# The last expert's product 128 rows wide, joined to the spreading product: attention and a soft mixture of experts on one core

## The chip, the cores and the metric

One Trainium2 chip, one core of it. The metric is device microseconds per execution; the kernel before takes 178.54 us (median of three runs, 178.18 to 178.70). One execution was profiled. An expert's weights are 4 MB as float32; the kernel casts them to 16 bits while loading.

## The reference

Windowed attention (8 batches, 8 heads, 576 positions, head size 64; half of the heads see the last 32 positions, half every fourth of the last 128) feeds a soft mixture of 8 experts with 4 slots each. What matters here is the second part, with x of 4608 rows and 512 columns:

```python
logits = x @ phi                              # 4608 x 32 slots
slot_input = softmax(logits, over rows).T @ x # 32 x 512
for e in range(8):
    h = maximum(slot_input[e] @ w1[e], 0)     # 4 x 1024
    slot_out[e] = h @ w2[e]                   # 4 x 512
return softmax(logits, over slots) @ slot_out # 4608 x 512
```

All of x must be seen before the experts can start, and all experts before the first row of the result.

## The kernel before

The order of the work on each engine is the order in which the program issues it (a manual schedule). A loop over the batches pipelines the attention by a hand-written list of steps; in it GpSimd (POOL) issues the loads of q, k, v and, between them, the weights. All these transfers and the outputs go through one software DMA queue, in order of issue. w1 of all experts and w2 of experts 0 to 2 are loaded during the loop. When the raw inputs of the last batch have been read (L550), their memory becomes the pool `w2b`: one transfer brings w2 of experts 3, 4 and 5 (3 MB as 16-bit numbers), and experts 6 and 7 go into the freed q/k slabs, first the columns 0 to 255 of both, then the columns 256 to 511; expert 7's come in two transfers each, chunks 0 to 3 and 4 to 7 (`load_half`, L216 to L220).

The hidden values are computed 32 columns per expert (`hps`, L608), transposed to `hT`, and copied to `hTm` (L620 for experts 0 to 3 on DVE, L623 for 4 to 7 on ACT). In `hTm` each expert has 32 columns, of which only its own 4 slots are not zero.

The second layer (`emit_so`, L635 to L648) multiplies, for each of 8 chunks of 128 hidden values, these 32 columns with the chunk of w2. A product fills 32 of the 128 columns of TensorE's array, and four products are put at four different column groups: experts 0 to 3 side by side, and for a single expert chunk c goes to rows 32*(c%4) of the accumulator `so`. So `so` holds four partial sums of the 32 slots. `gather_so` (DVE) copies half of its columns to `so_part` as 16-bit numbers; `spread_so` multiplies them with the constant `spread`, which adds the four partial sums and at the same time writes the sum to all four groups of 32 rows; ACT copies this to `so_sb`.

```python
so[row : row + 32, cols],
hTm[:, g, c, 32 * j : 32 * j + 32],
w2t[e][:, c, cols],
```

Then the output. `emit_fin` (L662) multiplies 128 rows of the exponentials ET (32 slots) with `so_sb`; the four row groups of `so_sb` serve four such blocks of a batch at four row groups of the array. The products go to `psum_f`, with four buffers. ACT (L673) and DVE (L677) take turns to scale a block into `om`. `emit_batch` does the four blocks of a batch and issues its output on POOL (L686). Six batches are written in two halves of the columns: `emit_so(0, ...)`, gather and spread for columns 0 to 255 come first; the loop over the six batches writes these columns, and expert 6's second half is put ahead of batch 2, expert 7's ahead of batch 4, the gather ahead of batch 5, the spread behind batch 5. Then come the second halves of the six batches, two whole batches, and the last 64 rows of each batch (`om_l`, L713).

Of the kernel before, what the change touches and what calls it, by code (L numbers as in the profile page):

```python
# [9 lines left out]
FP32 = mybir.dt.float32  # L10
FP16 = mybir.dt.float16
# [29 lines left out]
DH = DMODEL // 2  # L41
# [55 lines left out]
def kernel(  # L97
# [10 lines left out]
    nc = tc.nc  # L108
# [10 lines left out]
    spread = cst[:, o + 128 : o + 256]  # L119
# [10 lines left out]
    so_part = consts.tile([128, DMODEL], FP16, name="so_part")  # L130
    so_sb = consts.tile([128, DMODEL], FP16, name="so_sb")
    hTm = consts.tile([128, 2, 8, 128], FP16, name="hTm")
# [3 lines left out]
    w1t, w2t = {}, {}  # L136

    def weights_tile(pool, which, e0, e1):
        n = (4 * FDIM, 8 * DMODEL)[which - 1]
        t = pool.tile([128, e1 - e0, n], FP16, name=f"w{which}_{e0}", tag=f"w{which}_{e0}")  # L140
        for e in range(e0, e1):
            of = t[:, e - e0]
            if which == 1:
                w1t[e] = of.rearrange("p (c f) -> p c f", c=4)
            else:
                w2t[e] = of.rearrange("p (c n) -> p c n", c=8)
        return t
# [16 lines left out]
    def slab_weights(e, tag, n):  # L164
        t = fix.tile([128, n], FP16, name=f"w2_{e}", tag=tag)
        w2t[e] = t[:, 0 : 8 * DMODEL].rearrange("p (c n) -> p c n", c=8)
# [9 lines left out]
    ring = ctx.enter_context(tc.tile_pool(name="ring", bufs=2, space=bass.MemoryType.PSUM))  # L176
# [28 lines left out]
    def load_full(t, which, e0, e1):  # L205
        if which == 1:
            nc.gpsimd.dma_start(
                out=t.rearrange("p e (u x) -> p (e u) x", u=2),
                in_=moe_w1[e0:e1].rearrange("e (u p c) f -> p (e u) (c f)", u=2, p=128),
            )  # L210
        else:
            nc.gpsimd.dma_start(
                out=t, in_=moe_w2[e0:e1].rearrange("e (p c) n -> p e (c n)", p=128)
            )

    def load_half(e, s, n):  # L216
        src = moe_w2[e].rearrange("(p c) n -> p c n", p=128)
        cols = slice(DH * s, DH * s + DH)
        for u in range(0, 8, n):
            nc.gpsimd.dma_start(out=w2t[e][:, u : u + n, cols], in_=src[:, u : u + n, cols])  # L220
# [249 lines left out]
    for which in "QK":  # L470
        load_raw(which, 1)
    nc.gpsimd.dma_start(
        out=phi_raw.rearrange("p (u c) s -> p u (c s)", u=2),
        in_=moe_phi.rearrange("(u p c) s -> p u (c s)", u=2, c=2),
# [15 lines left out]
    def step(op, b):  # L490
        if op[0] in "ARM" and op[1:] in TILES:
            kind, i = TILES[op[1:]]
            if op[0] == "A":
                tmp[(op[1:], b)] = emit_av(b, kind, i)
            elif op[0] == "R":
                tmp[("R" + op[1:], b)] = emit_recip(b, kind, i, tmp[(op[1:], b)])
            else:
                engine = nc.scalar if op[1:] in ON_ACT else nc.vector
                norm_mult(b, kind, i, tmp.pop((op[1:], b)), tmp.pop(("R" + op[1:], b)), engine)
        elif op in ("S0", "S1", "S2"):  # L500
            tmp[(op, b)] = emit_scores(b, int(op[1]))
        elif op in ("E0", "E1", "E2"):
            emit_exp(b, int(op[1]), tmp.pop(("S" + op[1], b)))
        elif op in ("MK0", "MK1", "MK2"):
            emit_mask(b, int(op[2]))
        elif op[0:2] in ("QT", "KT", "VT"):
            turn(op[0], b, int(op[2]))
        elif op in ("XP0", "XP1"):
            tmp[(op, b)] = xT_plain(b, int(op[2]))
        elif op in ("XD0", "XD1"):  # L510
            tmp[(op, b)] = xT_dil(b, int(op[2]))
        elif op in ("XPc0", "XPc1", "XDc0", "XDc1"):
            xT_copy(b, op[1], int(op[3]), tmp.pop((op[0:2] + op[3], b)))
        elif op in ("VA", "VB", "VC", "VD"):
            tmp[(op, b)] = v_rows(b, "ABCD".index(op[1]))
        elif op in ("VAc", "VBc", "VCc", "VDc"):
            v_place(b, "ABCD".index(op[1]), tmp.pop((op[0:2], b)))
        elif op in ("LG", "EP"):
            tmp[(op, b)] = (back_logits if op == "LG" else back_erow)(b)
        elif op == "ET":  # L520
            back_et(b, tmp.pop(("LG", b)))
        elif op == "ER":
            back_er(b, tmp.pop(("EP", b)))
        else:
            {"ED": back_erd, "U": back_u, "UT": back_add}[op](b)

    def loads(which, b):
        load_raw(which, b)
        if which == "V":
            if b > 2:  # L530
                load_weights(1)
            if b == B - 1:
                load_weights(len(weights))
# [5 lines left out]
    w2b_pool = None  # L539
    for it in range(B + max(s for _, s in STEPS)):  # L540
        for op, stage in STEPS:
            b = it - stage
            if not 0 <= b < B:
                continue
            step(op, b)
            if op in frees and b + 2 < B:
                loads(frees[op], b + 2)
            left.discard((op, b))
            if w2b_pool is None and not left:
                raw_pool.release()  # L550
                w2b_pool = tc.alloc_tile_pool(name="w2b", bufs=1, side="right")
                late = weights_tile(w2b_pool, 2, 3, 6)
                slab_weights(6, "qk0", QK_SLAB)
                slab_weights(7, "qk1", QK_SLAB)
                load_full(late, 2, 3, 6)
                for s in range(2):
                    for e in (6, 7):
                        load_half(e, s, 8 if e == 6 else 4)
        if it == 0:
            nc.vector.tensor_copy(  # L560
                out=phi4, in_=phi_raw[:, :, None, :].broadcast_to([128, 4, 4, N_SLOTS])
            )
# [6 lines left out]
    h_pool = tc.alloc_tile_pool(name="hp", bufs=1)  # L569
# [33 lines left out]
    for fc in range(2):  # L603
        for g in range(2):
            for dc in range(4):
                for j in range(4):
                    e = 4 * g + j
# [4 lines left out]
                        start=(g == 0 and dc == 0),  # L612
                        stop=(g == 1 and dc == 3),
# [3 lines left out]
    for c in range(8):  # L617
# [3 lines left out]
        out=hTm[:, 0].rearrange("p c (j s) -> p c j s", j=4)[:, :, :, 0:16], in_=hT4[:, :, :, 0:16]  # L621
    )
    nc.scalar.copy(  # L623
        out=hTm[:, 1].rearrange("p c (j s) -> p c j s", j=4)[:, :, :, 16:32], in_=hT4[:, :, :, 16:32]
    )
    psum_e.release()
    psum_f = tc.alloc_tile_pool(name="psum_f", bufs=4, space=bass.MemoryType.PSUM)

# [6 lines left out]
    def emit_so(s, experts):  # L635
        cols = slice(0, DMODEL) if s is None else slice(DH * s, DH * s + DH)
        for c in range(8):
            for e in experts:
                g, j = divmod(e, 4)
                row = 32 * (j if len(experts) == 4 else c % 4)  # L640
                nc.tensor.matmul(
                    so[row : row + 32, cols],
                    hTm[:, g, c, 32 * j : 32 * j + 32],
                    w2t[e][:, c, cols],
                    start=(e < 4 and c == 0),
                    stop=(e == 7 and c > 3),
                    skip_group_check=True,
                )  # L648

    def gather_so(s):  # L650
        cols = slice(DH * s, DH * s + DH)
        nc.vector.tensor_copy(out=so_part[:, cols], in_=so[:, cols])

    def spread_so(s):
        cols = slice(DH * s, DH * s + DH)
        rep = ring.tile([128, DH], FP32, name=f"rep_{s}", tag="ring")
        nc.tensor.matmul(rep, spread, so_part[:, cols], start=True, stop=True)
        nc.scalar.copy(out=so_sb[:, cols], in_=rep)

    turn = [0]  # L660

# [19 lines left out]
    def emit_batch(b, c0, c1, n=4):  # L681
        dst = out[S * b : S * b + 512].rearrange("(j p) d -> p j d", p=128)
        for j0 in range(0, 4, n):
            for j in range(j0, j0 + n):
                emit_fin(et_cols(b)[0], j, c0, c1, om[b][:, j, c0:c1], 4 * b + j)
            nc.gpsimd.dma_start(  # L686
                out=dst[:, j0 : j0 + n, c0:c1], in_=om[b][:, j0 : j0 + n, c0:c1]
            )
# [2 lines left out]
    emit_so(None, (0, 1, 2, 3))  # L691
    for e in (4, 5):
        emit_so(None, (e,))
    for e in (6, 7):
        emit_so(0, (e,))
    gather_so(0)
    spread_so(0)
    for b in range(NHALF):
        if b in (2, 4):
            emit_so(1, ({2: 6, 4: 7}[b],))  # L700
        if b == 5:
            gather_so(1)
        emit_batch(b, 0, DH, 2 if b == 0 else 4)
    spread_so(1)
    for b in range(NHALF):
        emit_batch(b, DH, DMODEL)
    for b in range(NHALF, B):
# [4 lines left out]
    for e in range(2):  # L712
        nc.gpsimd.dma_start(  # L713
            out=rest[:, e, 512:576, :].rearrange("n i d -> i n d"), in_=om_l[64 * e : 64 * e + 64]
# [37 lines left out]
```

## Time and profile before

| | |
|---|---|
| median of three runs | 178.54 us |
| the profiled execution's own time | 178.29 us |
| its span, first to last instruction | 176.5 us |
| PE, DVE, ACT busy | 123.5, 126.0, 123.5 us |
| POOL busy | 38.4 us |
| read from and written to HBM | 62.07 and 9.44 MB |
| first output issued | 149.40 us |
| last two outputs issued from | 166.34 us |

The profile gives one page for an execution: the span in 40 slices, with each engine's busy tenths, the clock granted to TensorE (PEclk) and what the DMA engines moved; the chain of work that ended last; and groups of instructions by source line. Lnnn is a line of the kernel. The trace behind it can be asked for windows of time, for a tile's instructions, for waits, and for each DMA's time from issue to landing. All times below are microseconds from the start of the span.

### The profile page before, as it was taken

Reading aid. Unit: us, or ns where it says so; the run is one execution under the profiler, and the core shown is the slowest. Engines: PE = TensorE matmul, PEld = TensorE weight load, DVE = VectorE, ACT = ScalarE, POOL = GpSimd, SP = SyncE. Lnnn points to the kernel's source line nnn. Section 1 sums busy time; section 2 is a strip of 40 time slices with the busy share of each in tenths; the row PEclk is TensorE's granted clock in tenths of the full one; section 3 lists DMA queues with packets and bytes.
Section 4 is the critical chain, followed back from the end, with each engine's and each line's share of the span. In section 5 each row is a group of like instructions: output and inputs, shape, how many; then the busy total and the mean of one; then the engine's idle time right before and its main releaser. Section 6 shows DMA issues by size and latency. Waiting matters only on the chain.

```text
span 176.5 us, 4724 instructions
## 1 busy us (share of the span) xinstructions
PE 123.5 (70%) x2004; PEld 80.9 (46%) x2004; DVE 126.0 (71%) x275; ACT 123.5 (70%) x266; POOL 38.4 (22%) x60
## 2 busy tenths in 40 slices
PE   0026928998888888988989888978677295778300
PEld 0015616676566566656766557656332142221000
DVE  6473899999999999999999998465130104878500
ACT  6007758999999999999999999995501104888300
POOL 7321022112112112116000002710000001856600
PEclk9999999969999999999789999996858969655555
DMA  5999999999999999999999999999999999999997
GB/s 83 215 214 210 214 212 215 215 213 214 216 212 217 211 218 215 208 215 220 213 211 217 213 218 216 222 210 225 213 213 221 192 198 175 340 398 397 401 415 209
DMA packets 18981, 40.83 MB, mean 231 GB/s; under 512 B 1169, under 2 KB 11537, under 8 KB 18193
## 3 DMA queue, kind: packets, MB, share of 16 engines
q0 software_dynamic: 18816, 40.41, 113.8%
q8 instruction: 15, 0.25, 0.5%
q1 hardware_dynamic: 144, 0.14, 0.3%
q14 instruction: 6, 0.04, 0.1%
HBM read 62.07 MB, written 9.44 MB: 405 GB/s over the span
## 4 chain that ended last, share of the span: by engine, by line
ACT 38%; DMA 27%; DVE 14%; PE 10%; issue 2%; POOL 2%; POOLq 0%; ACTq 0%
DMA w<-in_moe_w_dram 19%; ACT p L282 10%; DMA phi_raw<-in_moe_phi_dram 8%; ACT vX L253 7%; ACT xp L337 7%; DVE qk L231 5%; PE f L664 5%; ACT om L673 3%; ACT xT L376 3%; ACT xT L378 3%; DVE p L293 3%; DVE vT L231 3%; ACT xd L337 2%; PE s L273 2%; PE rp L357 2%
## 5 line engine op out<-in xcount | busy, mean ns | idle before, releaser
L282 ACT ACTIVATE p<-s 128x1920 f16<-128x1920 f32 (+1 forms) x24 | 44.6, 1857 | 10.2 <-PE s L273 10.1
L273 PE MATMUL s<-qk 32*128 32x128 f16 (+2 forms) x704 | 26.7, 295 | 18.4 <-DVE qk L231 12.0
L253 ACT COPY vX<-rv 128x768 f16<-128x768 f16 (+1 forms) x32 | 27.8, 943 | 1.8 <-PE rv L247 1.8
L316 PEld LDWEIGHTS <-p 128*128 128x128 f16 (+1 forms) x480 | 22.4, 103 | 13.3 <-DVE xp L341 4.0
L337 ACT ACTIVATE xp<-o_P,rc_P 128x64 f16<-128x64 f32 x96 | 26.5, 497 | 2.2 <-DVE rc_P L328 2.2
L273 PEld LDWEIGHTS <-qk 32*128 32x128 f16 x704 | 17.3, 117 | 21.6 <-DVE qk L231 12.0
L293 DVE TENSOR_TENSOR p<-p,masks 128x1920 f16<-128x1920 f16 (+1 forms) x24 | 25.7, 1084 | 0.2
L231 DVE STREAM_TRANSPOSE qk<-rawQ 128x576 uint32<-128x576 uint32 x16 | 18.8, 1243 | 2.7 <-DMA rawQ<-in_q_dram 2.7
L316 PE MATMUL o_P<-vX,p 128*128 128x65 f16 (+1 forms) x288 | 20.0, 205 | 0.8 <-ACT xp L337 0.2
L231 DVE STREAM_TRANSPOSE qk<-rawK 128x576 uint32<-128x576 uint32 x16 | 19.5, 1231 | 0.4 <-DMA rawK<-in_k_dram 0.4
L247 PE MATMUL rv<-cst,vT 128*128 128x128 f16 x176 | 17.5, 242 | 3.2 <-DVE vT L231 1.8
L231 DVE STREAM_TRANSPOSE vT<-rawV 128x576 uint32<-128x576 uint32 x16 | 19.4, 1223 | 0.5 <-DMA rawV<-in_v_dram 0.5
L686 POOL DMA_DIRECT2D out_dram<-om x15 | 11.1, 744 | 39.2 <-DVE om L677 34.8
L247 PEld LDWEIGHTS <-vT 128*128 128x128 f16 x176 | 13.2, 124 | 7.5 <-issue 3.7
L677 DVE TENSOR_SCALAR om<-f,rrow 128x256 f16<-128x256 f32 (+1 forms) x28 | 13.5, 519 | 3.5 <-PE f L664 2.9
L664 PE MATMUL f<-so_sb,ET 32*128 32x256 f16 (+1 forms) x60 | 12.5, 392 | 3.9 <-ACT om L673 2.7
L673 ACT ACTIVATE om<-f,rrow 128x256 f16<-128x256 f32 (+1 forms) x28 | 12.8, 503 | 2.6 <-PE f L664 2.0
L376 ACT COPY xT<-rp 128x576 f16<-128x576 f16 x16 | 11.5, 909 | 1.3 <-PE rp L357 1.3
L316 PE MATMUL o_D<-vX,p 128*128 128x65 f16 x128 | 9.9, 202 | 2.5 <-DVE xp L341 2.0
L201 POOL DMA_DIRECT2D rawQ<-in_q_dram x8 | 5.1, 633 | 29.4 <-DVE rc_P L328 18.4
L378 ACT COPY xT<-rd 128x576 f16<-128x576 f16 x16 | 10.6, 795 | 0.0
L341 DVE TENSOR_TENSOR xd<-o_D,rc_D 128x256 f16<-128x256 f32 x24 | 9.9, 412 | 0.2
(81 smaller groups left out, 176.7 us busy)
## 6 DMA issues: line engine op xcount, KB each, us to landing
w<-in_moe_w_dram POOLq DMA_DIRECT2D x3, 3072.0 KB, 35.5
out_dram<-om POOLq DMA_DIRECT2D x11, 512.0 KB, 4.6
w<-in_moe_w_dram POOLq DMA_DIRECT2D x5, 1024.0 KB, 15.9
rawQ<-in_q_dram POOLq DMA_DIRECT2D x8, 576.0 KB, 12.7
rawK<-in_k_dram POOLq DMA_DIRECT2D x8, 576.0 KB, 11.4
rawV<-in_v_dram POOLq DMA_DIRECT2D x8, 576.0 KB, 11.6
out_dram<-om POOLq DMA_DIRECT2D x2, 1024.0 KB, 7.3
w<-in_moe_w_dram POOLq DMA_DIRECT2D x2, 512.0 KB, 36.7
```

The source lines that it names most:

```text
L231: nc.vector.transpose(out=out_, in_=in_)
L247: nc.tensor.transpose(rg[:, n_t, :, c, :], rows, ident)
L253: copy(out=vX[b % 2][:, t0 : t0 + n, :, 0:D], in_=rg.rearrange("p n h c d -> p n h (c d)"))
L273: nc.tensor.matmul(sps[:, h, c0 : c0 + w], kk, qq, start=(tt == 0), stop=(tt == 1))
L282: return nc.scalar.activation(out=pt, in_=sps[:, :, 0:n], func=AF.Exp, scale=SCALE)
L293: return nc.vector.tensor_tensor(out=pt, in0=pt, in1=m, op=ALU.mult)
L316: nc.tensor.matmul(o[rows, h, :], lhs, rhs, start=(n == 0), stop=(n == len(jobs) - 1), skip_group_check=True,)
L337: nc.scalar.activation(out=dst[:, h], in_=src[:, h], func=AF.Copy, scale=rc[:, h : h + 1])
L376: copy(out=xT_t[b][:, c, :], in_=rg[:, 0:S])
L378: copy(out=xT_t[b][:, 2 + c, :].rearrange("p (i r) -> p i r", r=DIL), in_=rg[:, :, 0:SUB].rearrange("p r i -> p i r"),)
L664: nc.tensor.matmul(fp[:, 0 : c1 - c0], ET[32 * j : 32 * j + 32, m : m + 128], so_sb[32 * j : 32 * j + 32, c0:c1], start=True, stop=True,)
L673: nc.scalar.activation(out=dst, in_=fp[:, 0 : c1 - c0], func=AF.Copy, scale=rrow[:, blk : blk + 1])
```

## The change

Three things are done.

First, the transfer of w2 of experts 3, 4 and 5 becomes two: expert 3 alone, then 4 and 5.

Second, a tile `hT7` holds expert 7's hidden columns four times side by side, so that its products are 128 wide: each fills all columns of the array and writes the same 32 sums to all four row groups.

Third, expert 7 leaves `emit_so`. `gather_so` now gathers the other seven experts and issues the spreading product at once, into an accumulation that it leaves open; `last_so` adds expert 7's eight products to it and copies the sum to `so_sb`. For the columns 0 to 255 the two stand one after the other ahead of the first batch. For the columns 256 to 511 expert 6 and the gather stand ahead of batch 2, and `last_so` behind batch 3.

```diff
-                late = weights_tile(w2b_pool, 2, 3, 6)
+                late = {x: weights_tile(w2b_pool, 2, *x) for x in ((3, 4), (4, 6))}
...
-                load_full(late, 2, 3, 6)
+                for x, t in late.items():
+                    load_full(t, 2, *x)
...
+    hT7 = h_pool.tile([128, 8, 4, 32], FP16, name="hT7", tag="hT7")
+    nc.vector.tensor_copy(out=hT7, in_=hTm[:, 1, :, None, 96:128].broadcast_to([128, 8, 4, 32]))
...
-                    stop=(e == 7 and c > 3),
+                    stop=(e == 6 and c > 3),
...
+    rep = {}
 
     def gather_so(s):
         cols = slice(DH * s, DH * s + DH)
         nc.vector.tensor_copy(out=so_part[:, cols], in_=so[:, cols])
 
-    def spread_so(s):
+        rep[s] = ring.tile([128, DH], FP32, name=f"rep_{s}", tag="ring")
+        nc.tensor.matmul(rep[s], spread, so_part[:, cols], start=True, stop=False)
+
+    def last_so(s):
         cols = slice(DH * s, DH * s + DH)
-        rep = ring.tile([128, DH], FP32, name=f"rep_{s}", tag="ring")
-        nc.tensor.matmul(rep, spread, so_part[:, cols], start=True, stop=True)
-        nc.scalar.copy(out=so_sb[:, cols], in_=rep)
+        for c in range(8):
+            nc.tensor.matmul(
+                rep[s],
+                hT7[:, c].rearrange("p a s -> p (a s)"),
+                w2t[7][:, c, cols],
+                start=False,
+                stop=(c == 7),
+            )
+        nc.scalar.copy(out=so_sb[:, cols], in_=rep[s])
...
-    for e in (6, 7):
-        emit_so(0, (e,))
+    emit_so(0, (6,))
     gather_so(0)
-    spread_so(0)
+    last_so(0)
     for b in range(NHALF):
-        if b in (2, 4):
-            emit_so(1, ({2: 6, 4: 7}[b],))
-        if b == 5:
+        if b == 2:
+            emit_so(1, (6,))
             gather_so(1)
         emit_batch(b, 0, DH, 2 if b == 0 else 4)
-    spread_so(1)
+        if b == 3:
+            last_so(1)
```

## The prediction

> **What bounds the kernel now.** I read the page first, its slices in time above all:
>
> ```profile
> PE   0026928998888888988989888978677295778300
> DMA  5999999999999999999999999999999999999997
> GB/s 83 215 214 210 214 212 215 215 213 214 216 212 217 211 218 215 208 215 220 213 211 217 213 218 216 222 210 225 213 213 221 192 198 175 340 398 397 401 415 209
> ```
>
> The DMA row is full from the second slice to the last, while every engine has gaps. So whatever the change does to an engine must be asked twice: does it move the end of the DMA stream? Next, the chain of waits over the stretch that the change edits:
>
> ```profile
> 112.33 34.05 DMA w<-in_moe_w_dram
> 146.37 0.04 issue
> 146.41 0.32 PE so L641 x4
> ...
> 146.76 0.43 DVE so_part L652
> ...
> 147.23 0.28 PE rep L657
> ...
> 147.54 0.38 ACT so_sb L658
> ...
> 147.96 0.31 PE f L664 x4
> ```
>
> Read alone, this says that from the landing of expert 7's second quarter (146.37) to so_sb (147.92) lie 1.55 us, of which gather and spreading product are some 0.8. Then DMA by stretches of time (last two numbers: DMA share, GB/s):
>
> ```profile
> 140.00:149.00 9.00, 5.68 (x68) 2.71 (x68) 1.07 (x3) 1.11 (x3) 0.00 (x0) 0.81 1.42 193
> 149.00:149.50 0.50, 0.50 (x8) 0.11 (x7) 0.50 (x2) 0.50 (x3) 0.10 (x1) 1.00 0.96 130
> 149.50:150.00 0.50, 0.50 (x12) 0.21 (x12) 0.50 (x2) 0.43 (x2) 0.50 (x1) 1.00 0.76 101
> 150.00:150.50 0.50, 0.39 (x4) 0.17 (x3) 0.29 (x2) 0.37 (x1) 0.50 (x2) 1.00 0.63 86
> 150.50:151.00 0.50, 0.34 (x2) 0.18 (x2) 0.50 (x2) 0.50 (x3) 0.50 (x2) 1.00 1.31 232
> 151.50:166.00 14.50, 10.87 (x54) 2.85 (x53) 12.24 (x25) 11.37 (x24) 9.01 (x13) 0.50 1.97 396
> ```
>
> There is a trough between the weights and the outputs, about 1 us deep. It looks like the prize, but the packet records of the trace show who idles in it. Each transfer ends with 16 four-byte completion writes, one per DMA engine. Nine engines write their last of the weights by 149.9; seven go on, the last until 151.41. That slowest engine then completes the outputs at 152.06, 152.71, 154.01, 155.31, 156.62, 157.94 and so on to 174.78: 0.65 us per 256 KB and 1.31 per 512 KB throughout, the pace of the full stream. It never waits for an output, and it ends last. So the end is its weights plus its share of the outputs; an earlier first output fills the trough of the other nine only. What counts for the end is that no output comes late for the slowest engine. POOL issues them so:
>
> ```profile
> 149.40 3.03 POOL L686 DMA_DIRECT2D out_dram<-om  x4 [33.97 <-DVE om L677]
> 152.63 0.74 POOL L686 DMA_DIRECT2D out_dram<-om  x1 [0.19 <-issue]
> 153.95 0.74 POOL L686 DMA_DIRECT2D out_dram<-om  x1 [0.57 <-ACT om L673]
> 155.06 0.75 POOL L686 DMA_DIRECT2D out_dram<-om  x1 [0.37 <-issue]
> ```
>
> The first packet of an output starts at 150.68, 1.28 us after its issue. The slack of an output is thus the slowest engine's previous completion less issue plus 1.28: 0.7 us for the first three, 1.0 for batch 2, 1.4 for batch 3 and 1.39 for batch 4 (issued 153.95, wanted 156.62 - 1.28 = 155.34).
>
> **The change part by part.** *w2 of expert 3 alone.* One more POOL issue, 0.77 us (the row of L212). It pushes expert 6's first half from 106.34 to 107.1; POOL then idles 4.3 us until 111.58 in any case, and the transfers wait some 34 us in the queue, which hides it. Without that cover it would cost 0.77. On the stream: two 256 KB pieces take the slowest engine 2.68 us where one 512 KB piece takes 2.65, so 0.03. Expert 3 lands at about 131 (126.47, the landing before, plus a third of the 14.6 us to 141.1). So the 32 products of experts 0 to 3 run at 138.44 and no longer wait until 141.15.
>
> *hT7.* A DVE copy of 128x1024, bounded by the 128x512 copies: 2 x 0.29 (L560) to 2 x 0.42 (L620); I take 0.8, as it stands next to the latter. It waits for ACT's copy (139.0) and ends by 139.9; DVE has no other work until the gather, 144.2 now, and the first reader starts at 145. Hidden.
>
> *Join ahead of the landing, columns 0 to 255.* Expert 6's half lands at 143.73 (106.34 + 37.4), its products end by 144.15, gather 0.43, spread 0.28: done at 144.9, before expert 7's quarters (145.04 and 146.37). After the second quarter four products are left. They are 128 wide, and where before four 32-wide ones started within 0.02 us of each other (146.41 to 146.43), these take turns: 256 columns are 0.107 us each at full clock, 0.213 at half (512 columns: groups start 0.213 and 0.427 apart). With the tail of 0.17 that is 0.59 or 1.02, so_sb ends at 147.41 or 147.84 instead of 147.91: 0.50 or 0.07 earlier. By the slowest engine this is worth 0.0.
>
> *Columns 256 to 511.* Here it costs. Expert 7's eight products were two groups, 0.43 us at half clock; now they are eight turns, 1.71. They stand behind batch 3 in PE's queue, ahead of batch 4's products, and the copy to so_sb now stands ahead of batch 4 on ACT (0.37). And at batch 2, PE's queue holds the spreading product, which waits for a gather that DVE reaches only behind batch 1's evictions; batch 2's products stand behind it. The later gather, product and copy after batch 5 go away, but there the queue has slack.
>
> *Which clock.* Granted clock in the gate's own stretches (PE busy, clock):
>
> ```profile
> 140.87:144.28 3.41, 3.13 (x32) 0.50 1.45 197
> 144.28:147.70 3.42, 2.04 (x38) 1.00 1.45 198
> 147.70:151.11 3.41, 2.35 (x23) 1.00 1.13 164
> 151.11:154.52 3.41, 2.55 (x19) 0.50 1.92 389
> ```
>
> The clock of a stretch follows the array work of the one before, counted as columns times the filled share of the array: 2,944 (144.28 to 147.70) kept it full; 2,769 (31.64 to 35.06) and 1,472 (147.70 to 151.11) lost it. After the change the stretch from 140.87 holds experts 4, 5 and 6 alone: 16 x 128 + 8 x 64 = 2,560, so it should be half from 144.28.
>
> [...]
>
> *The sum at half clock.* With rows of before (evictions 0.37 apart on ACT and 0.41 on DVE, 0.47 long; POOL 0.53 behind the last eviction, as 153.42 to 153.95): batch 1's evictions and the gather end at 150.45; spread, then batch 2's products from 150.8, evicted 151.2 to 152.1; batch 3 152.1 to 153.05; the eight products 152.37 to 154.07; their tail and the copy end at 154.65; batch 4 is evicted by 155.49 and issued at 156.02, 0.68 after 155.34. If the clock is full again from 147.70 to 151.11, the same steps give 155.56, 0.22 late; full throughout, 154.29, 1.05 early. The same chain for before gives 153.79 (153.95 in the trace). Outputs behind batch 4 keep 0.3 us or more. I take the middle of the two half-clock cases, 0.45: the profiled execution's 178.29 (span 176.5 and 1.8 around it) + 0.45 + 0.03 = 178.77; its time stands 0.25 below the median of the three runs, so 179.0 beside 178.54. Bounds: nothing to 0.9 late, by the 0.2 us of drift in that chain.
>
> **The rivals.** *No change, 178.5.* Batch 4 comes in time: full clock, or slack that the chain counts too small. For it: the other free-running stretches could begin elsewhere; the slack at half clock is missed by only 0.2 to 0.7. It decides at an issue of 155.34.
>
> *The first output decides: faster, 178.0.* If the end follows the nine engines that idle in the trough, so_sb's 0.50 at full clock is gained; the whole trough, 0.96, is the limit (177.6). For it: 86 GB/s at 150.0. Against: the completions of the slowest engine, without a gap.
>
> *Weight loads of 128 columns show.* If the eight loads of 0.10 us (L657's) don't run beside the products, batch 4 is 0.8 later still: 178.54 + 0.45 + 0.8 = 179.8. Against: transposes at L357 start 0.055 apart with a load of 128 columns each.
>
> **How the numbers follow.** About 0.3%, 0.54 us, can be told from no change. Batch 4 late: 0.52, of which 0.31 above 0.54 and 0.21 below. Loads show: 0.12, all slower. No change: 0.18. First output decides: 0.18, of which 0.13 beyond 0.54. Slower 0.31 + 0.12 = 0.43; same 0.21 + 0.18 + 0.05 = 0.44; faster 0.13. The range 178.0 to 179.7 leaves out most of the loads' case and the deep end of the faster one; the likeliest case alone gives 178.5 to 179.4.
>
> **What would show it.** Right: PE clock 0.5 in 144.3 to 147.7; eight products at the new line between batch 3 and 4 taking about 1.7 us; batch 4's output issued after 155.3; a dip of GB/s near 156 to 157; the landing of the last weight at 151.7 as before. Wrong: clock full there, or batch 4 issued before 155 with no dip (no change); a stream that ends 0.5 earlier with the same landing of the weights (first output decides). A last weight landing that moves by itself would upset every step, since all is counted from it.

## The result, and the profile after

The changed kernel takes 179.63 us (median of six, 179.35 to 180.08) against 178.29 for the kernel before on the same chip (178.11 to 178.70): 1.0075 times as long, 95% interval 1.0055 to 1.0094. That is 1.34 us slower. The profiled execution took 179.35 us, with a span of 177.6.

The path that the change was cut for did get shorter. The chain of waits after the change, from the landing of expert 7's second quarter on:

```profile
146.06 0.04 issue
146.11 1.03 PE rep L665 x4
147.13 0.02 issue
147.16 0.38 ACT so_sb L672
147.54 0.04 issue
...
149.91 0.44 DVE so_part L657
150.35 0.04 issue
150.40 0.37 PE rep L660
150.77 0.37 PE f L678 x3
...
152.46 1.82 PE rep L665 x8
```

From the landing to the end of the copy to so_sb it is now 1.48 us instead of 1.55: gather and spreading product are gone from it, but the four 128-wide products take 1.03 instead of 0.32. Further down stand the two new waits: the gather and the spreading product ahead of batch 2 (149.91 to 150.77), and eight products, 1.82 us, ahead of batch 4. What they do to the outputs shows in POOL's instructions after the change:

```profile
149.07 2.17 POOL L700 DMA_DIRECT2D out_dram<-om  x3 [21.94 <-DVE om L691]
152.57 0.75 POOL L700 DMA_DIRECT2D out_dram<-om  x1 [1.32 <-ACT om L687]
153.51 0.75 POOL L700 DMA_DIRECT2D out_dram<-om  x1 [0.20 <-issue]
156.07 0.74 POOL L700 DMA_DIRECT2D out_dram<-om  x1 [1.82 <-ACT om L687]
157.01 0.74 POOL L700 DMA_DIRECT2D out_dram<-om  x1 [0.20 <-ACT om L687]
```

The first output is issued earlier (149.07 instead of 149.40, though only 0.02 earlier against the landing of the last weight, of which more below), but batch 2's only at 152.57 (before, the last of the four issues from 149.40, at 151.69) and batch 4's at 156.07 (before: 153.95). After each of them the DMA stream has a hole. Stretches of time after the change, DMA share and GB/s last:

```profile
151.50:153.00 1.50, 1.35 (x7) 0.68 (x7) 1.41 (x4) 1.31 (x4) 0.43 (x1) 0.50 1.91 387
153.00:153.50 0.50, 0.50 (x4) 0.36 (x3) 0.00 (x0) 0.00 (x0) 0.31 (x1) 0.50 1.14 223
153.50:154.00 0.50, 0.50 (x4) 0.23 (x2) 0.00 (x0) 0.00 (x0) 0.49 (x1) 0.50 0.46 96
154.00:156.50 2.50, 1.83 (x13) 0.65 (x12) 1.75 (x4) 2.02 (x6) 0.68 (x2) 0.50 1.98 403
156.50:157.00 0.50, 0.40 (x3) 0.14 (x2) 0.45 (x2) 0.50 (x2) 0.32 (x1) 0.50 0.14 19
157.00:157.50 0.50, 0.49 (x3) 0.20 (x3) 0.42 (x2) 0.41 (x2) 0.49 (x1) 0.50 0.28 66
157.50:166.00 8.50, 7.32 (x31) 1.56 (x28) 7.53 (x15) 7.68 (x16) 5.45 (x8) 0.50 1.98 400
```

Before the change there was no such hole between 151.5 and 166. By the completion writes in the packet records, the slowest engine stood still for 0.36 us ahead of batch 2's output and for 0.89 us ahead of batch 4's.

The trace's landing times sum it up in one number per kernel, the time from the last weight's landing to the last output's landing: 151.70 to 175.23 before, 23.53 us; 151.38 to 176.28 after, 24.90 us. The outputs take 1.37 us longer, and the profiled execution is 1.06 slower because its weights happened to land 0.32 earlier. I use this length, called the output phase, for all experiments below.

| kernel | median us | ratio to before (95%) | output phase, us |
|---|---|---|---|
| before | 178.29 | | 23.53 |
| the change | 179.63 | 1.0075 (1.0055 to 1.0094) | 24.90 |
| first half of the columns alone | 178.15 | 0.9993 (0.9984 to 1.0002) | 23.54 |
| second half alone | 179.70 | 1.0077 (1.0061 to 1.0092) | 25.24 |
| expert 3 alone | 178.16 | 0.9996 (0.9987 to 1.0004) | 23.54 |
| eight products behind batch 5 | 179.89 | 1.0083 (1.0062 to 1.0103) | 25.26 |
| join and products behind batch 5 | 179.73 | 1.0069 (1.0048 to 1.0089) | 24.23 |
| eight products more | 181.95 | 1.0201 (1.0182 to 1.0220) | 27.76 |
| fillers that keep the clock | 179.85 | 1.0069 (1.0045 to 1.0092) | 26.12 |
| five fillers ahead of the first output | 179.13 | 1.0050 (1.0028 to 1.0072) | 23.90 |
| ten fillers there | 181.08 | 1.0148 (1.0132 to 1.0164) | 26.67 |
| one more copy on ACT | 178.42 | 1.0002 (0.9990 to 1.0014) | 23.79 |
| four more copies on ACT | 179.13 | 1.0051 (1.0030 to 1.0072) | 24.58 |
| ten products at PE's very end | 179.42 | 1.0067 (1.0046 to 1.0089) | 24.43 |

The phase is of the profiled execution alone, the medians and ratios are of all. The kernel before was timed beside each group anew, with medians from 178.29 to 178.45.

### The profile page after: what moved, and what is told of

Its sections match the earlier page's. It is cut to its first block, busy times and chain, and to the rows that moved or that the text cites. A ratio compares the mean times of both kernels' runs of the same rounds, so it can differ in the third digit from the quotient of the medians.

```text
span 177.6 us, 4725 instructions
## 1 busy us (share of the span) xinstructions
PE 124.0 (70%) x2004; PEld 81.9 (46%) x2004; DVE 126.7 (71%) x276; ACT 123.6 (70%) x266; POOL 38.9 (22%) x61
## 4 chain that ended last, share of the span: by engine, by line
ACT 39%; DMA 27%; PE 16%; DVE 8%; POOL 2%; issue 2%; POOLq 0%
DMA w<-in_moe_w_dram 19%; ACT p L282 10%; DMA phi_raw<-in_moe_phi_dram 8%; ACT vX L253 8%; ACT xp L337 8%; PE f L678 5%; ACT xT L376 4%; ACT om L687 3%; ACT xT L378 3%; DVE vT L231 3%; PE s L273 2%; ACT xd L337 2%; PE rp L357 2%; DVE qk L231 2%; PE rv L247 2%
## 5 line engine op out<-in xcount | busy, mean ns | idle before, releaser
L282 ACT ACTIVATE p<-s 128x1920 f16<-128x1920 f32 (+1 forms) x24 | 45.4, 1890 | 10.1 <-PE s L273 10.0
L253 ACT COPY vX<-rv 128x768 f16<-128x768 f16 (+1 forms) x32 | 28.6, 978 | 1.8 <-PE rv L247 1.8
L337 ACT ACTIVATE xp<-o_P,rc_P 128x64 f16<-128x64 f32 x96 | 27.2, 526 | 2.0 <-DVE rc_P L328 2.0
L337 ACT ACTIVATE xd<-o_D,rc_D 128x64 f16<-128x64 f32 x32 | 9.4, 559 | 1.3 <-DVE rc_D L328 1.3
```

The costliest lines, as they stand in the source:

```text
L253: copy(out=vX[b % 2][:, t0 : t0 + n, :, 0:D], in_=rg.rearrange("p n h c d -> p n h (c d)"))
L282: return nc.scalar.activation(out=pt, in_=sps[:, :, 0:n], func=AF.Exp, scale=SCALE)
L337: nc.scalar.activation(out=dst[:, h], in_=src[:, h], func=AF.Copy, scale=rc[:, h : h + 1])
```

## The experiments

My theory: the end is the slowest DMA engine's stream, which an earlier first output can't shorten, and the loss is the late outputs of batches 2 and 4. Its rivals: the first output decides; the loss is in the first half or in the loads; TensorE's clock has no part in it.

### The three parts by themselves

First half of the columns as changed, second half as before (edits against the changed kernel):

```diff
-                    stop=(e == 6 and c > 3),
+                    stop=(e == (6 if s == 0 else 7) and c > 3),
...
-        if b == 2:
-            emit_so(1, (6,))
+        if b in (2, 4):
+            emit_so(1, ({2: 6, 4: 7}[b],))
+        if b == 5:
             gather_so(1)
         emit_batch(b, 0, DH, 2 if b == 0 else 4)
-        if b == 3:
-            last_so(1)
+    spread_so(1)
```

> Only the columns 0 to 255 and the loads as in the change; the columns 256 to 511 as before (expert 6 ahead of batch 2, expert 7 in 32-wide products ahead of batch 4, gather ahead of batch 5). Theory, late outputs of batches 2 and 4: no loss is left, since neither the join ahead of batch 2 nor the eight products ahead of batch 4 are there, and no gain either, since the slowest DMA engine reads weights until about 151.1 to 151.4 whatever the first output does: within 0.2 us of before, 178.1 to 178.5. Rival, the first output decides: so_sb is ready 0.4 earlier, 177.9. Rival, the loss is from the first half or the loads: 179 or more.

The reverse, the first half as before and the second as changed:

```diff
...
-    emit_so(0, (6,))
+    for e in (6, 7):
+        emit_so(0, (e,))
     gather_so(0)
-    last_so(0)
...
+        if s == 0:
+            nc.scalar.copy(out=so_sb[:, cols], in_=rep[s])
```

> The reverse: the columns 0 to 255 as before (expert 7 in 32-wide products, gather and spread behind the landing), the loads and the columns 256 to 511 as changed. Theory, late outputs: the whole loss is here, 1.0 to 1.8 us, 179.3 to 180.1, with a stop of the outputs near 156.5 to 157.3. Rival, the loss is from the first half: within 0.3 us of before, 178.0 to 178.6.

And the kernel before with expert 3's weights loaded alone:

```diff
-                late = weights_tile(w2b_pool, 2, 3, 6)
+                late = {x: weights_tile(w2b_pool, 2, *x) for x in ((3, 4), (4, 6))}
```

> The kernel before with w2 of expert 3 loaded alone, and nothing else. Theory: 0.03 us more for one more transfer, hidden otherwise: 178.2 to 178.5. The landing of expert 7's last quarter stays within 0.3 of 151.5, although its issue moves from 114.7 to some 126. Rival, the split costs by that late issue: slower by over 0.3 us.

Measured: 178.15, 179.70 and 178.16 us, the first two in their ranges and the third 0.04 below its own. The whole loss is in the second half of the columns; the first half and the split cost nothing that can be told. The first half alone is also the clean test of the first output. POOL's instructions in it:

```profile
148.60 2.18 POOL L704 DMA_DIRECT2D out_dram<-om  x3 [21.45 <-DVE om L695]
151.22 0.75 POOL L704 DMA_DIRECT2D out_dram<-om  x1 [0.44 <-ACT om L691]
152.16 0.74 POOL L704 DMA_DIRECT2D out_dram<-om  x1 [0.19 <-issue]
153.63 0.74 POOL L704 DMA_DIRECT2D out_dram<-om  x1 [0.73 <-ACT om L691]
```

Its first output comes 2.79 us ahead of the last weight's landing (151.39), where before it was 2.30 ahead of it: half a microsecond gained, and the output phase is 23.54 instead of 23.53. (In the change's own profiled execution the first output was 2.31 ahead, almost as before: there the clock was half from 142.84 on, here it was full from 141.85 to 148.67.) So an earlier first output is worth nothing here, and the rival "the first output decides" is out.

### How much slack the first outputs have

If an earlier first output gains nothing, a later one should cost only what exceeds the slack. In the kernel before, n copies that nothing reads were put on ACT behind the copy to so_sb:

```diff
         nc.scalar.copy(out=so_sb[:, cols], in_=rep)
+        if s == 0:
+            scr = h_pool.tile([128, DH], FP16, name="scr", tag="scr")
+            for _ in range(n):      # n = 1, n = 4
+                nc.scalar.copy(out=scr, in_=rep)
```

> The kernel before with one more copy of the spreading product to a scratch tile, which nothing reads, on ACT behind the copy to so_sb of columns 0 to 255. It delays ACT's evictions, and so the first outputs, by 0.37, whatever TensorE's clock. Theory, the slowest DMA engine decides: the slack of 0.6 to 0.7 covers it, no change, 178.1 to 178.5. Rival, the first output decides: 0.37 slower, 178.7.

> The same with four such copies: the first outputs 1.48 later. Theory: 1.48 less the slack of 0.62 to 0.73, so 0.75 to 0.9 slower, 179.1 to 179.3, the rest hidden. Rival, the first output decides: 1.5 slower, 179.8.

Measured: no change with one copy (1.0002, at most 0.25 us by the interval), 179.13 with four, 0.8 us by the medians and 0.9 by the ratio, as expected. The rival's 0.37 for one copy is outside the interval. So is its 1.5 for four; but in that trace the first output itself came only 1.08 later, which the interval (0.54 to 1.28 us) does not exclude, so it is the one copy that speaks against the rival, with the first half alone. And the traces correct the size of the slack. With four copies the third output is issued 1.22 us later, against the last weight's landing, than before, and lands 0.94 later: a slack of 0.28, where I had 0.62. With one copy it is 0.42 later and lands 0.18 later: 0.24. So a cost of about 0.2 us was to be expected even of one copy, which the interval allows.

The same question was first put with products on PE, five or ten of 512 columns that nothing reads, between the spreading product and the first output products. `filler(n, columns)` issues n such products; without a second number they have 512 columns.

```diff
...
     gather_so(0)
     spread_so(0)
+    filler(5)      # or 10
```

> The kernel before with five products of 512 columns, which nothing reads, on PE between the spreading product of columns 0 to 255 and the first output products. At full clock they take 5 x 0.213 = 1.07 us from 147.34 and delay the first output by about 0.45. Theory, the slowest DMA engine decides: the first outputs have 0.6 to 0.7 slack, so no change, 178.1 to 178.5. Rival, the first output decides: 0.45 slower, 178.75.

> The same with ten such products: 2.13 us, the first output about 1.5 later. Theory: the slack of 0.6 to 0.7 is used up and the rest is paid, 0.8 to 0.9 slower, 179.1 to 179.2. Rival, the first output decides: 1.5 slower, 179.8. Rival, the outputs catch up: no change.

Both missed: 179.13 and 181.08. With five, the times spread from 178.54 to 180.71, and the profiled execution is the fastest of them; what held the others up isn't known (their clock at the fillers was not seen). With ten, 181.08 is some 1.9 us more than expected. Two causes are in its trace: the first output came 2.18 later against the last weight, not 1.5, and one output landed some 1.0 us late behind a sixteenth packet of instruction fetch, which is taken up below. For the slack, both traces agree with the copies on ACT: the third output is issued 0.56 and 2.18 later and lands 0.31 and 1.94 later, a slack of 0.25 and 0.24.

### Where the late products stand, and how many

In the changed kernel, the eight products and the copy moved from behind batch 3 to behind batch 5, with the join left ahead of batch 2:

```diff
         emit_batch(b, 0, DH, 2 if b == 0 else 4)
-        if b == 3:
-            last_so(1)
+    last_so(1)
```

> The changed kernel with the eight products and the copy of columns 256 to 511 moved from behind batch 3 to behind batch 5; the join stays ahead of batch 2. Theory: batch 4 is in time, batch 2 stays 0.2 late, and the eight products now stand ahead of the second halves, whose first output has about 0.4 too little slack: 178.5 to 178.9, some 0.7 to 1.1 less than the change. Rival, the join ahead of batch 2 is the cost: as slow as the change, 179.6.

Missed: 179.89, where the rival had put it. But the join alone is not the cost: batch 2's hole stays as it was in the change (its output lands 0.45 late, there 0.43). Batch 4 is in time, as expected (issued at 154.94, and the stream is full from 154 to 159), and its hole has moved to the first second half, which is issued at 158.98. Stretches of time in this kernel:

```profile
153.50:154.00 0.50, 0.47 (x4) 0.18 (x4) 0.42 (x2) 0.41 (x2) 0.48 (x1) 0.50 0.38 78
154.00:159.00 5.00, 3.72 (x20) 1.59 (x20) 2.65 (x7) 2.58 (x7) 1.77 (x4) 0.50 1.98 403
159.00:159.50 0.50, 0.50 (x3) 0.20 (x3) 0.39 (x1) 0.41 (x2) 0.50 (x1) 0.50 0.64 111
159.50:160.00 0.50, 0.33 (x4) 0.08 (x2) 0.24 (x1) 0.50 (x2) 0.30 (x2) 0.50 0.00 0
```

Then the join was moved too, back to where it was before the change, ahead of batch 5:

```diff
         if b == 2:
             emit_so(1, (6,))
+        if b == 5:
             gather_so(1)
         emit_batch(b, 0, DH, 2 if b == 0 else 4)
-        if b == 3:
-            last_so(1)
+    last_so(1)
```

> The changed kernel with join and eight products of columns 256 to 511 both moved: gather ahead of batch 5 as in the kernel before, spread, eight products and copy behind batch 5. Theory, late outputs: batches 2 and 4 are in time again; the eight products end near 155.8 and the copy near 156.2, so that the first second half is issued near 158.0 where about 157.6 is wanted: 0.3 to 0.6 slower than before, 178.6 to 178.9, one stop of the outputs near 159. Rival, the 128-wide products cost the same wherever they stand: 179.5 or more.

The profiled execution (178.94) does as expected: no hole until 158, the first second half issued at 158.15, one short hole, output phase 24.23.

```profile
152.00:154.00 2.00, 1.05 (x7) 0.27 (x7) 1.18 (x3) 0.39 (x1) 1.28 (x2) 0.50 1.99 404
...
158.50:159.00 0.50, 0.42 (x3) 0.10 (x2) 0.13 (x2) 0.44 (x2) 0.39 (x1) 0.50 0.72 139
159.00:159.50 0.50, 0.41 (x4) 0.12 (x4) 0.42 (x2) 0.43 (x2) 0.41 (x1) 0.50 0.09 18
159.50:162.00 2.50, 1.99 (x12) 0.53 (x12) 2.35 (x6) 2.31 (x6) 1.61 (x3) 0.50 1.97 404
```

But only two of seven executions were like this; five took 179.69 to 179.90, and none of those was profiled. So the median is 179.73, which is where the rival had put it, and what adds 0.8 us in most executions stays open. In the profiled one the clock was full from 143.36 to 150.19, where the change had it at half; whether the five had half clock there isn't shown (their mean clock over the span, 0.865 to 0.874 against 0.856 and 0.873 of the two, doesn't tell). What the two profiled moves do show is that the holes follow the products: they come ahead of whichever output stands behind them.

Eight more products of the same size, ahead of the eight in the changed kernel:

```diff
...
         if b == 3:
+            filler(8, 256)
             last_so(1)
```

> The changed kernel with eight more products of 256 columns, 128 wide, that nothing reads, just ahead of expert 7's eight behind batch 3. At half clock they take 1.71 us. Theory: batch 4's output comes 1.7 later and all of it is paid: 181.3. Rival, the loss has another place: 179.6.

Measured 181.95, 2.3 us over the change and 0.65 over what was expected. In the trace batch 4's output is issued 1.75 us later than in the change (158.15, with the weights landing 0.33 later), and the stream stands still for over 2 us from 157. The phase is 2.86 longer: 1.75, and 1.1 with the one late output that the ten fillers had shown too.

### The clock

In the changed kernel, products that nothing reads were put into PE's waits, to keep the granted clock up:

```diff
...
+    filler(8)
     emit_so(0, (6,))
+    filler(3)
     gather_so(0)
     last_so(0)
...
             emit_so(1, (6,))
+            filler(3, 256)
             gather_so(1)
         emit_batch(b, 0, DH, 2 if b == 0 else 4)
+        if b in (0, 1, 2):
+            filler(2, 256)
```

> The changed kernel with products that nothing reads in PE's waits: eight of 512 columns ahead of expert 6's first half, three ahead of expert 7, three of 256 while the gather ahead of batch 2 runs, two of 256 behind each of batches 0 to 2. Theory: the clock is full from 144 to 153 or so, the eight products take 0.9 instead of 1.7, and batch 4 is issued near 154.5 to 155 instead of 156.07: 178.3 to 178.8. Rival, the clock has no part in it: 179.6 or, as the fillers stand in the queue, slower.

The total, 179.85, says nothing, since the fillers themselves delay the first output by 1.15 us and bring the sixteenth packet of instruction fetch once more. The trace does. The clock in two stretches of this kernel (PE busy, clock):

```profile
146.80:150.20 3.40, 2.67 (x21) 1.00 1.23 167
150.20:153.70 3.50, 3.12 (x29) 1.00 1.21 236
```

and its products into `rep` (shortest, middle and longest in ns):

```profile
L665 PE MATMUL rep<-w,hT x16: 272/272/283, 147.5 to 154.1; 128*128 128x256 f16 x16
```

The same two views of the changed kernel:

```profile
142.84:146.26 3.42, 2.00 (x14) 0.50 1.45 196
146.26:149.67 3.41, 2.42 (x20) 0.50 1.30 176
149.67:153.08 3.41, 2.33 (x17) 0.50 1.62 313
153.08:156.50 3.42, 2.75 (x17) 0.50 1.63 332
```

```profile
L665 PE MATMUL rep<-w,hT x16: 373/418/418, 144.8 to 153.9; 128*128 128x256 f16 x16
```

At full clock the eight products take 1.05 us (153.36 to 154.41) instead of 1.82, and batch 4's output follows batch 3's by 1.61 us (from 154.49 to 156.10) instead of 2.56. There is no hole at batch 4, although that alone proves little, since batches 0 to 3 land later in this kernel too (by 0.66 to 1.45) and so leave batch 4 more slack. So the half clock makes some 0.95 us of batch 4's lateness, as an estimate from two traces whose earlier outputs differ. These traces don't divide up the rest; in the change, 1.19 us of batch 4's 2.44 is there at batch 2's issue already, ahead of the eight products.

## Why the prediction was right, and too small

*The bound.* Right, and shown: the phase stays 23.54 with a first output half a microsecond earlier.

*The loads.* Right: 0.9996, nothing to be told. The landing of expert 7's last quarter is at 151.53 there.

*hT7.* Right, and cheaper than taken: it ran from 137.86 to 138.28, 0.42 us where I had 0.8, and nothing waited for it.

*The first half.* Its two values were 0.50 and 0.07 earlier; 0.07 it was (1.48 instead of 1.55): the clock was half, and the products started 0.213 apart (0.17 after the first). The spacing of 512-column groups at full clock is 0.216 in the trace of before, where the prediction had 0.213.

*The clock.* Right in kind: half from 142.84, behind the stretch from 139.43 that holds experts 4 and 5. By the count of the prediction that stretch had 16 x 128 = 2,048 columns. I had expected a stretch from 140.87 with 2,560; where the stretches begin differs from execution to execution, and the second half alone had one of exactly 2,560, from 140.71, and lost the clock too. But the count gives no sharp bound. By the products that start in a stretch, the clock stayed full in the trace of before behind all 23 full-clock stretches of 2,894 or more and was lost behind all six of 2,769 or fewer; in the change it stayed full behind one of 2,375 (from 43.86) and was lost behind 2,163, 2,184 and 2,048. With 2,769 lost in the one and 2,375 kept in the other, half clock at 2,560 was a guess that came true. And I took the middle of two half-clock cases; it was the one with half clock to the end, which I had at 0.68.

*The sum.* This is the step that failed in size. The account for batch 4's output, all against the last weight's landing:

- Predicted 2.07 us later than before; it was 2.44 (4.69 behind that landing, where before it was 2.25). The chain drifted by 0.37. Of that, 0.22 is there when the gather ends (150.35, where 150.45 was predicted with a landing 0.32 later). The likely reason, not tested, is that at half clock a batch's third and fourth products wait for buffers of the batch before: batch 1's start at 148.51 and 148.56, then 148.88 and 148.95.
- Predicted slack 1.39; it landed 1.23 late, so it was 1.21. Issue plus 1.28 was the first packet of any engine; after both holes the slowest engine's completion, less its 1.31 for the output, puts its own start 1.44 behind the issue, which is 0.16 of the 0.18.
- Batch 2, for which the chain had left 0.10, was 0.43 late by itself; that is part of the 1.23.

So from 0.45: to 0.68 by the clock, 0.37 by the chain, 0.18 by the slack, which gives 1.23, and 0.14 elsewhere in the phase: 1.37. The slack is also what the ACT copies measured, 0.24 to 0.28 for the third output where I had 0.62; the later start explains 0.16 of that, and the rest stays open.

*The range.* The time is above the 178.5 to 179.4 that the likeliest case alone gave. It is inside the range because that left room for the rival of the weight loads, which fell; so much was luck.

*The rivals.* No change fell with the two holes; the first output with the first half alone. The third, that weight loads of 128 columns show, fell too, although its 179.8 is the nearest to the measured time: the eight products start 0.21 apart, the 0.213 of 256 columns at half clock, with nothing added.

## What to carry to other kernels

Here, where transfers fill the time from end to end, a first output half a microsecond earlier gained nothing (a phase of 23.54 instead of 23.53), since the slowest DMA engine did not wait for it; so find that engine's completions first. Then list every later output with its own slack: with the slack of batch 4 gone, eight more products ahead of it were paid in full (issued 1.75 us later, the phase 2.86 longer with the other late output). And here one product that fills the whole array stands for one of four that shared it: eight took 1.82 us at half clock and 1.05 at full, where four that shared it had started within 0.02 us of each other. The work that it saves elsewhere has to be weighed against these turns, at the clock that will be granted there.

## What the runs showed of the hardware that I had not expected

**A sixteenth packet of instruction fetch came with 1.2 us more.** Ten fillers (twenty more instructions on PE, a weight load and a product each) had brought a sixteenth 16 KB packet of instruction fetch at 165.1, and the runs with eight more products and with the fillers that keep the clock, sixteen and forty instructions more, behaved alike. To measure it alone, ten products that delay nothing were put at the end of PE's work in the kernel before:

```diff
...
+    filler(10, 64)
     rest = out.rearrange("(n e s) d -> n e s d", e=2, s=S)
```

> The kernel before with ten products of 64 columns, which nothing reads, behind the last output product on PE, where PE has nothing else to do. They delay no output. In the runs with twenty more instructions on PE the trace showed a sixteenth fetch of 16 KB of instructions, at 161.6 to 166.5, and one DMA engine ending some 1.1 us behind the others. Theory: that fetch holds one DMA engine up, 1.0 to 1.2 us slower, 179.3 to 179.6. Rival, the late engine comes from something else: no change, 178.3.

Measured 179.42, 1.0067 times before (1.0046 to 1.0089), 1.2 us. The page of this kernel has a packet more in the queue of instructions:

```profile
q8 instruction: 16, 0.26, 0.5%
```

and the last stretches of the span, DMA share and GB/s last, have a tail:

```profile
173.50:174.00 0.50, 0.00 (x0) 0.00 (x0) 0.00 (x0) 0.00 (x0) 0.00 (x0) 0.50 1.51 430
174.00:174.50 0.50, 0.00 (x0) 0.00 (x0) 0.00 (x0) 0.00 (x0) 0.00 (x0) 0.50 0.77 197
174.50:175.00 0.50, 0.00 (x0) 0.00 (x0) 0.00 (x0) 0.00 (x0) 0.00 (x0) 0.50 0.12 33
175.00:175.50 0.50, 0.00 (x0) 0.00 (x0) 0.00 (x0) 0.00 (x0) 0.00 (x0) 0.50 0.10 29
```

There were 15 such packets before, and after the change too, so the fetch has no part in the result. The sixteenth starts at 166.43 and takes 1.04 us; the output that lands next needs 2.33 us behind its predecessor instead of 1.34, and at the end a trickle of 30 GB/s runs for a microsecond after the other engines are done (before, the last two of these stretches had 12 and 0 GB/s). In all four runs with the sixteenth packet the first or second output to land after its start needs 2.33 to 2.40 us; in the ten with fifteen no 512 KB output does, except those issued late. So twenty more instructions on PE, which delay no output, cost this kernel 1.2 us, and what its trace shows with them is the one packet more at 166.43. Why the next output is late behind it, and whether a packet at another time would cost as much, the runs don't show.

**One issue of POOL waited 12 us.** With one transfer more, POOL issued expert 7's last quarter not at 114.67 but here (the kernel before with expert 3 alone):

```profile
111.29 3.12 POOL L220 DMA_DIRECT2D w<-in_moe_w_dram  x4 [3.81 <-PE s L273]
126.58 0.74 POOL L220 DMA_DIRECT2D w<-in_moe_w_dram  x1 [12.17 <-DMA w<-in_moe_w_dram]
```

The profile puts 12.17 us of POOL's idle time before it down to the landing of weights. In the trace of the change the same issue, at 126.39 behind 12.03 us, comes 0.29 behind the landing (126.10) of the transfer issued at 81.25, the oldest of eight then under way; what sets that wait isn't shown. It cost nothing here, where the queue still held 24 us of work; a shorter queue was not tried. I had not counted that wait.
